# Retention followed by a gated unit: half of every second unit's convolution on VectorE, ScalarE and GpSimd, unit steps one pass later

## The chip, the cores and the metric

The kernel runs on one core of one Trainium2 chip. The metric is the device time of one execution in microseconds (us). The kernel before took 168.69 us as the median of three runs (168.61 to 168.87). Each profile shows one execution, and its durations belong to that execution alone.

## What is computed

The first part is retention (attention without a softmax, with a decay per head); the second a gated linear unit on its output, with a causal convolution of five taps as the gate:

```
scores = (q @ k.T) / sqrt(64)                 # 8 batches, 8 heads, 576 tokens, 64 per head
ret = scores * gamma[h] ** (i - j)            # for i >= j, else 0
x = (ret @ v), heads side by side             # 8 x 576 x 512
gate = sigmoid(sum over t of conv_w[t] * x shifted by 4 - t tokens)    # per channel
out = (gate * (x @ w_val)) @ w_out            # 8 x 576 x 512, float32
```

## The kernel before, in words

The tokens are cut into 36 chunks of 128: four full chunks for each batch, and, after every four batches, two chunks that hold the last 64 tokens of two batches each. Two successive chunks make a unit, so there are 18 units, numbered n; unit n has the chunks 2n and 2n+1. The decay is split into a factor per key token, put on V (`cast_v`, GpSimd, line 221), and a factor per query token, put on the result (`take_x`, VectorE, lines 331 and 337).

For a chunk the steps are these. `turn_k` (line 246) turns K on TensorE (line 241) into the PSUM bank `tps` and copies it to SBUF as `kt` (line 249). `scores` (line 280) multiplies K by Q into two banks; `masks` (line 289) evacuates each of the two with the causal mask. `carried` (lines 304, 310) adds what earlier chunks left in the state; `values` (line 321) adds masked scores times V; `take_x` stores the result as bf16 `xg`, with channels on the partitions, in four blocks of 128 channels. `update` (line 352) adds the chunk to the state and `take_state` (line 363, two ScalarE casts) copies the state to SBUF. The queries of a batch are loaded together, cast (`cast_q`, line 234), and turned by `turn_q` (lines 241 and 263) in four parts, one part a pass as a rule. In the main loop `turn_q` uses the same PSUM bank `tps` as `turn_k`; its pool has one buffer.

For a unit the steps are `conv` (line 385), `gate` (line 393), `value` (line 400, and the product with the gate on VectorE, line 403) and `project` (line 411, the copy on ScalarE, line 414, and the store, lines 417 and 420). `conv` runs five taps over four blocks as 64 x 64 diagonal matrices: 40 matmuls of 256 columns into two of the three PSUM banks of the pool `g`. `value` and `project` come in two halves, each with one bank of that pool.

The order is written out by hand, and every engine runs its instructions in that order. A prologue treats the chunks 0 to 3 and the units 0 and 1 with steps in single file and, where TensorE would idle, with matmuls on zeros (`keep_warm`, line 445). Then a loop over t = 4 to 37 (line 542) makes one pass a chunk: loads and casts ahead, `take_state(t)`, `scores(t+1)`, the first mask, `values(t)`, and then, in even passes, `take_x(t)`, the second mask, `conv(n)` and gates, `turn_k(t+2)`, two `value` halves with a `turn_q` between them; in odd passes `turn_k(t+2)` first, then `take_x(t)` and the second mask, then two `project` halves with a `turn_q` between them. Both end with `carried(t+1)` and `update(t+1)`. Unit n has its conv in pass 2n+2 and its projection in pass 2n+3. K is loaded by GpSimd's DMA queue four chunks ahead, V and Q by SyncE's (SP), which carries the stores too.

Of the kernel before, what the change touches and what calls it, by code (L numbers as in the profile page):

```python
# [13 lines left out]
F32 = mybir.dt.float32  # L14
BF16 = mybir.dt.bfloat16
# [6 lines left out]
def kernel(  # L22
# [48 lines left out]
    with tc.manual_schedule():  # L71
# [118 lines left out]
        mask_t = consts.tile([P, P], BF16, name="maskt")  # L190

        wvb = consts.tile([P, NP, NP, P], BF16, name="wvb")
        dg = consts.tile([P, NP, KC, 64], BF16, name="dg")
        cw = consts.tile([P, KC * NP], F32, name="cw")

# [23 lines left out]
        def cast_v(t, eng=nc.gpsimd):  # L219
            vb = bfp.tile([P, H, D], BF16, name="vb")  # L220
            eng.tensor_tensor(vb, loaded["v", *chunks[t]],  # L221
                                    gin[:, chunks[t][2], :].unsqueeze(2).to_broadcast([P, H, D]), op=ALU.mult)
            vbf[t] = vb
# [28 lines left out]
        def turn_q(job, copy=nc.scalar.copy, pool=None):  # L252
            ps = turned(qbf[job], pool)
            if job[0] == "own":
                qt = tp_sb.tile([P, NP, P], BF16, name="qt")
                qtd["own", job[1]] = qt
                dst = qt
            else:
                b, r = job[1:]
                if ("batch", b) not in qtd:  # L260
                    qtd["batch", b] = tp_sb.tile([P, NP, RQ, P], BF16, name="qtb", bufs=2)
                dst = qtd["batch", b][:, :, r, :]
            copy(dst, ps)  # L263
# [9 lines left out]
        def scores(t, spare=False):  # L273
            kt = ktd[t]
            s = [ps_g.tile([P, NP, P], F32, name="g") if spare else ps_s.tile([P, NP, P], F32, name=f"s{i}")
                 for i in range(2)]
            for pr in range(NP):
                for i in range(2):
                    r = slice(i * 64, i * 64 + 64)
                    nc.tensor.matmul(s[i][:, pr, :], lhsT=kt[r, pr, :], rhs=queries(t, r, pr),  # L280
                                     start=(pr == 0), stop=(pr == NP - 1), skip_group_check=True)
            sps[t] = s
# [84 lines left out]
        def xs(n, rows, blk, shift):  # L367
            kind, b, c = chunks[2 * n]
            x = xg[b // GB]
            if kind == "full":  # L370
                c0 = c * P + shift
                return x[rows, b % GB, blk, c0:c0 + 2 * P]
            c0 = NCH * P + shift
            return x[rows, :, blk, c0:c0 + TAIL]

        gps, gsb, zsb = {}, {}, {}

        def conv(n):
            g = [ps_g.tile([P, 2, 2 * P], F32, name="g") for _ in range(2)]
            lo, hi = slice(0, 64), slice(64, 128)  # L380
            for pr in range(2):
                a, b = 2 * pr, 2 * pr + 1
                for kk in range(KC):
                    for (rows, blk, cols, bank) in ((lo, a, lo, 0), (hi, b, lo, 1), (lo, b, hi, 0), (hi, a, hi, 1)):
                        nc.tensor.matmul(g[bank][cols, pr, :], lhsT=dg[rows, blk, kk, :], rhs=xs(n, rows, blk, kk),  # L385
                                         start=(pr == 0 and kk == 0), stop=(pr == 1 and kk == KC - 1),
                                         skip_group_check=True)
            gps[n] = g
            gsb[n] = []

        def gate(n, i):
            t = gp.tile([P, 2, 2 * P], F32, name=f"gate{i}")
            nc.scalar.activation(t, gps[n][i], AF.Sigmoid)  # L393
            gsb[n].append(t)

        def value(n, i):
            vps = ps_g.tile([P, 2, 2 * P], F32, name="g")
            for j in range(2):
                for o in range(NP):
                    nc.tensor.matmul(vps[:, j, :], lhsT=wvb[:, o, 2 * i + j, :], rhs=xs(n, slice(0, P), o, PAD),  # L400
                                     start=(j == 0 and o == 0), stop=(j == 1 and o == NP - 1), skip_group_check=True)
            z = gp.tile([P, 2, 2 * P], BF16, name=f"z{i}")
            nc.vector.tensor_tensor(z, gsb[n][i], vps, op=ALU.mult)  # L403
            zsb[n, i] = z

        def project(n, i):
            kind, b, c = chunks[2 * n]
            last = n == NT // 2 - 1
            o = ps_g.tile([P, DM], F32, name="g")
            for j in range(NP):  # L410
                nc.tensor.matmul(o, lhsT=zsb[n, j // 2][:, j % 2, i * P:(i + 1) * P], rhs=wob[:, j, :],  # L411
                                 start=(j == 0), stop=(j == NP - 1))
            ob = op_sb.tile([P, DM], F32, name="ob")
            nc.scalar.copy(ob, o)  # L414
            if kind == "full":
                c0 = (c + i) * P
                nc.sync.dma_start(out=out[b, c0:c0 + P, :], in_=ob)
            else:
                for j in range(2):
                    (nc.scalar if last and j else nc.sync).dma_start(out=out[b + 2 * i + j, NCH * P:S, :], in_=ob[j * TAIL:(j + 1) * TAIL])  # L420
# [40 lines left out]
        for (r, copy) in ((1, s_copy), (2, v_copy), (0, s_copy)):  # L461
            turn_q(("batch", 0, r), copy, ps_g)
        turn_q(("batch", 0, 3), v_copy)
        scores(0)
        masks(0, 0)
        masks(0, 1)
        turn_k(1, s_copy)
        cast_v(0)
        cast_v(1)
        load_keys(4)  # L470
        carried(0)
        update(0)
        take_state(0)
# [9 lines left out]
        prep_wv(s_copy, 0)  # L483
        prep_wv(g_copy, 1)
        cast_v(2)
        for t in sbl:
            nc.gpsimd.memset(t, 0.0)
        keep_warm(2, turn_bank=True)
        values(1)
        take_x(1)  # L490
# [7 lines left out]
        gate(0, 1)  # L498
        value(0, 0)
        cast_v(3)  # L500
        load_keys(5)
        load_wo()
        values(2)
        take_x(2)
        update(2)
# [9 lines left out]
        take_x(3)  # L515
        update(3)
        take_state(3)
        keep_warm(3, turn_bank=True)
        for (r, copy) in ((0, g_copy), (1, g_copy), (2, s_copy), (3, g_copy)):
            cast_q(("batch", 1, r), copy)  # L520
        cast_v(4)
        load_keys(6)
        conv(1)
        gate(1, 0)
        gate(1, 1)
        turn_k(4, s_copy)
        value(1, 0)
        turn_q(("batch", 1, 0), v_copy)
        turn_q(("batch", 1, 1), s_copy, ps_g)
        turn_q(("batch", 1, 2), v_copy)  # L530
        turn_q(("batch", 1, 3), s_copy, ps_g)
        carried(4)
# [1 line left out]
        scores(4)  # L534
        masks(4, 0)
        masks(4, 1)
        turn_k(5)
        value(1, 1)
        load_keys(7)
        cast_v(5)  # L540

        for t in range(4, NT + 2):
            n = t // 2 - 1
            unit = n < NT // 2
            odd = t % 2 == 1
            jobs = qjobs.get(t, [])
            for b in qload.get(t, []):
                load_queries(b)
            if ok(t + LA - 2):
                load(t + LA - 2)  # L550
            if ok(t + 4):
                load_keys(t + 4)
            if ok(t + 2):
                cast_v(t + 2)
            for job in qjobs.get(t + 1, []):
                cast_q(job)
            if ok(t):
                take_state(t)
            if ok(t + 1):
                scores(t + 1)  # L560
                masks(t + 1, 0)
            if ok(t):
                values(t)
                if not odd:
                    take_x(t)
            if ok(t + 1) and not odd:
                masks(t + 1, 1)
            if unit and not odd and n > 1:
                conv(n)
                gate(n, 0)  # L570
                gate(n, 1)
            if ok(t + 2) and t > 4:
                turn_k(t + 2)
            if ok(t) and odd:
                take_x(t)
            if ok(t + 1) and odd:
                masks(t + 1, 1)
            part = project if odd else value
            if unit and t > 4:
                part(n, 0)  # L580
            if t == 4:
                project(0, 0)
            if jobs:
                turn_q(jobs[0])
            if unit and t > 4:
                part(n, 1)
            if t == 4:
                turn_k(6)
                project(0, 1)
            for job in jobs[1:]:  # L590
                turn_q(job)
            if ok(t + 1):
                carried(t + 1)
                update(t + 1)
            if t == 5:
                nc.gpsimd.tensor_copy(mask_t, mask)
                nc.gpsimd.memset(mask_t[0:64, 64:128], 0.0)
# [1 line left out]
_INS = ['q', 'k', 'v', 'moe_w_val', 'moe_conv_w', 'moe_w_out']  # L599
_OUTS = [((8, 576, 512), 'float32')]  # L600
# [25 lines left out]
```

## Time and profile before

| | before |
|---|---|
| median of 3 runs | 168.69 us |
| the profiled execution | 168.61 us |
| its span, first to last instruction | 166.7 us |
| granted TensorE clock | 0.998 |
| data moved | 35.23 MB, mean 211 GB/s |
| K load, issue to landing | 4.1 / 7.0 / 10.8 us (least, median, most) |

The span begins with the first instruction and ends with the last; the 1.9 us that are left lie around it. Where engines are given as shares, TensorE's matmuls are PE and its weight loads PEld, VectorE is DVE, ScalarE ACT, GpSimd POOL. A line such as "L249 DVE COPY kt<-tps" names the line of the kernel, the engine, the operation, and the tile written and read. In a timeline the first number is the start and the second the duration in us; brackets at the end give the engine's idle time before the instruction and what ended it. In a chain a row has the start, the time in us, and the work.

### The profile page before, as it was taken

The page shows a single profiled execution, that of the slowest core. Times are in us where ns is not written, and L with a number is a line of the kernel's source. Part 1 is how long each engine was busy: PE and PEld are TensorE (multiplying, and loading weights), DVE is VectorE, ACT ScalarE, POOL GpSimd, SP SyncE. Part 2 cuts the span into 40 slices and gives each one's busy share as a digit, 9 for nine tenths or more (in the row PEclk, how much of TensorE's full clock was granted, in tenths as well). Part 3 has the DMA queues.
Part 4 walks back from the last instruction along what each step waited for, and adds up shares of the span by engine and source line. Part 5 has one row for each costly group of instructions (what it writes and reads, how often), then busy time and mean ns, then how long its engine had stood idle before and what let it go on. Part 6 is the DMA issues. An engine that isn't in the chain of part 4 may idle for free.

```text
span 166.7 us, 5543 instructions
## 1 busy us (share of the span) xinstructions
PE 153.5 (92%) x2297; PEld 110.2 (66%) x2297; DVE 114.2 (68%) x217; ACT 89.9 (54%) x183; POOL 99.4 (60%) x132
## 2 busy tenths in 40 slices
PE   6768878799999999999999999999999999999970
PEld 1344656556868777777868686868686877868630
DVE  6784673676677777768677777777777788686330
ACT  6934337446655557474546556565555563554430
POOL 7596999279699378675379286537977462000000
PEclk9999999999999999999999999999999999999999
DMA  5999999998999999999999999999999991303204
GB/s 112 301 264 253 294 213 288 226 162 238 275 263 287 247 236 214 174 258 267 267 163 246 268 274 188 216 285 289 233 259 187 212 236 42 130 0 130 97 33 126
DMA packets 93958, 35.23 MB, mean 211 GB/s; under 512 B 80090, under 2 KB 88814, under 8 KB 93934
## 3 DMA queue, kind: packets, MB, share of 16 engines
q1 hardware_dynamic: 57744, 29.63, 67.7%
q0 software_dynamic: 36000, 4.98, 44.0%
q8 instruction: 18, 0.29, 0.8%
q10 hardware_dynamic: 190, 0.27, 0.6%
q14 instruction: 6, 0.05, 0.1%
HBM read 30.42 MB, written 9.44 MB: 239 GB/s over the span
## 4 chain that ended last, share of the span: by engine, by line
PE 83%; ACT 4%; DVE 3%; POOL 3%; DMA 2%; issue 2%; ACTq 0%; DVEq 0%; POOLq 0%
PE g L400 18%; PE g L411 18%; PE g L385 13%; PE tps L241 10%; PE o L321 7%; PE s L280 7%; PE st L352 4%; PE o L304 3%; DMA fkc<-in_k_dram 2%; PE tps L445 1%; POOL dg L202 1%; ACT qtb L263 1%; DVE p L289 1%; DVE kt L249 1%; ACT ob L414 1%
## 5 line engine op out<-in xcount | busy, mean ns | idle before, releaser
L289 DVE TENSOR_TENSOR p<-s,maskq 128x512 bf16<-128x512 f32 x62 | 42.2, 685 | 17.6 <-PE s L280 17.5
L221 POOL TENSOR_TENSOR vb<-fvc,gin 128x512 bf16<-128x512 f32 x36 | 37.7, 1046 | 22.0 <-DMA fvc<-in_v_dram 9.0
L403 DVE TENSOR_TENSOR z<-gate,g 128x512 bf16<-128x512 f32 x36 | 24.7, 687 | 20.8 <-PE g L400 20.8
L400 PE MATMUL g<-xg,wvb 128*128 128x256 bf16 x288 | 36.9, 273 | 0.0
L411 PE MATMUL g<-wob,z 128*128 128x512 bf16 x144 | 36.5, 379 | 0.3 <-DVE z L403 0.3
L414 ACT COPY ob<-g 128x512 f32<-128x512 f32 x36 | 21.1, 585 | 28.3 <-PE g L411 28.0
L393 ACT ACTIVATE gate<-g 128x512 f32<-128x512 f32 x36 | 19.5, 594 | 19.1 <-PE g L385 19.1
L400 PEld LDWEIGHTS <-wvb 128*128 128x128 bf16 x288 | 26.6, 98 | 3.3 <-issue 0.6
L96 POOL DMA_DIRECT2D kb<-in_k_dram x30 | 28.4, 946 | 0.1
L234 POOL CAST qb<-fqb 128x512 bf16<-128x512 f32 x28 | 17.0, 620 | 13.1 <-DMA fqb<-in_q_dram 13.1
L385 PE MATMUL g<-xg,dg 64*64 64x256 bf16 x720 | 23.2, 271 | 0.0
L363 ACT CAST sbd<-st 64x256 bf16<-64x256 f32 x48 | 17.6, 366 | 8.8 <-PE st L352 8.3
L331 DVE TENSOR_TENSOR xg<-o,gout 128x512 bf16<-128x512 f32 x31 | 21.1, 681 | 1.3 <-PE o L321 1.3
L385 PEld LDWEIGHTS <-dg 64*64 64x64 bf16 x720 | 18.4, 106 | 2.3 <-issue 0.8
L411 PEld LDWEIGHTS <-z 128*128 128x128 bf16 x144 | 12.5, 98 | 10.4 <-DVE z L403 1.2
L263 ACT COPY qtb<-tps 128x512 bf16<-128x512 bf16 x24 | 14.1, 588 | 4.2 <-PE tps L241 4.2
L241 PE MATMUL tps<-ident,kb 128*128 128x128 bf16 x144 | 14.5, 224 | 0.8 <-DVE kb L216 0.8
L280 PE MATMUL s<-qtb,kt 64*128 64x128 bf16 x248 | 12.3, 219 | 2.5 <-DVE kt L249 1.1
L249 DVE COPY kt<-tps 128x512 bf16<-128x512 bf16 x33 | 14.0, 423 | 0.9 <-PE tps L241 0.7
L321 PE MATMUL o<-p,vb 128*64 128x128 bf16 x280 | 14.5, 225 | 0.0
L241 PEld LDWEIGHTS <-qb 128*128 128x128 bf16 x144 | 10.6, 98 | 5.4 <-issue 1.4
L352 PE MATMUL st<-vb,kb 128*128 128x128 bf16 x128 | 12.4, 219 | 0.7 <-POOL vb L221 0.7
(71 smaller groups left out, 142.0 us busy)
## 6 DMA issues: line engine op xcount, KB each, us to landing
fqb<-in_q_dram SPq DMA_DIRECT2D x8, 1024.0 KB, 9.3
fvc<-in_v_dram SPq DMA_DIRECT2D x32, 256.0 KB, 8.8
out_dram<-ob SPq DMA_DIRECT2D x32, 256.0 KB, 5.7
kb<-in_k_dram POOLq DMA_DIRECT2D x30, 128.0 KB, 7.5
wvf<-in_moe_w_val_dram SPq DMA_DIRECT2D x1, 1024.0 KB, 7.4
fqc<-in_q_dram SPq DMA_DIRECT2D x8, 128.0 KB, 5.2
fvc<-in_v_dram SPq DMA_DIRECT2D x8, 128.0 KB, 5.0
out_dram<-ob SPq DMA_DIRECT2D x6, 128.0 KB, 3.3
```

Source lines behind the costliest of these rows:

```text
L96: nc.gpsimd.dma_start(out=kb, in_=k[b, :, c * P:(c + 1) * P, :].rearrange("h p d -> p h d"))
L221: eng.tensor_tensor(vb, loaded["v", *chunks[t]], gin[:, chunks[t][2], :].unsqueeze(2).to_broadcast([P, H, D]), op=ALU.mult)
L241: nc.tensor.transpose(ps[:, pr, :], flat[:, pr * P:(pr + 1) * P], ident)
L280: nc.tensor.matmul(s[i][:, pr, :], lhsT=kt[r, pr, :], rhs=queries(t, r, pr), start=(pr == 0), stop=(pr == NP - 1), skip_group_check=True)
L289: nc.vector.tensor_tensor(p, sps[t][i], m.unsqueeze(1).to_broadcast([P, NP, P]), op=ALU.mult)
L321: nc.tensor.matmul(o[r, pr, :], lhsT=vb[:, 2 * pr + i, :], rhs=pt[t, i][:, pr, :], start=(fresh and pr == 0), stop=(pr == NP - 1), skip_gr ...
L331: nc.vector.tensor_tensor(by_token(x[:, bl, :, PAD + i0:PAD + i0 + P]), ops[t].rearrange("p o (r n) -> p o n r", r=RQ), by_token(gout[:, : ...
L385: nc.tensor.matmul(g[bank][cols, pr, :], lhsT=dg[rows, blk, kk, :], rhs=xs(n, rows, blk, kk), start=(pr == 0 and kk == 0), stop=(pr == 1 a ...
L400: nc.tensor.matmul(vps[:, j, :], lhsT=wvb[:, o, 2 * i + j, :], rhs=xs(n, slice(0, P), o, PAD), start=(j == 0 and o == 0), stop=(j == 1 and ...
L403: nc.vector.tensor_tensor(z, gsb[n][i], vps, op=ALU.mult)
L411: nc.tensor.matmul(o, lhsT=zsb[n, j // 2][:, j % 2, i * P:(i + 1) * P], rhs=wob[:, j, :], start=(j == 0), stop=(j == NP - 1))
L414: nc.scalar.copy(ob, o)
```

## The change

In the even units from 2 to 16, `conv` on TensorE does only the first pair of blocks (20 matmuls). Block 2 is computed by five VectorE instructions (`tap`), block 3 by five ScalarE activations with a scale per channel, of which four go to a tile `tap` (two buffers) and are added by GpSimd. Taps are spread over the passes 2n+1, 2n+2 and 2n+3; the last ones stand at the head of pass 2n+3. The gate of such a unit is made in four halves instead of two whole instructions, and its blocks 2 and 3 are in natural channel order, for which there are second copies of the weights (`wvn`, `won`). Every unit from 2 on has its conv and `value` one pass later (2n+3) and its `project` in 2n+4. `take_x` and the second mask stand directly behind `values` in every pass, and `turn_k` copies on ScalarE in the passes 2n+2 and 2n+3 of these units. In the prologue some steps trade places and engines.

```
+        wvn = consts.tile([P, NP, 2, P], BF16, name="wvn")
+        won = consts.tile([P, 2, DM], BF16, name="won")
...
+        aside = set(range(2, NT // 2, 2))
+        acc = {}
+
+        def tap(eng, n, i, kk):
+
+            if kk == 0:
+                acc[n, i] = gp.tile([P, 2 * P], F32, name=f"acc{i}")
+            x = xs(n, slice(0, P), 2 + i, kk)
+            a = acc[n, i]
...
+            w = cw[:, kk * NP + 2 + i:kk * NP + 3 + i]
+            if i == 1:
+
+                t = a
+                if kk:
+                    t = gp.tile([P, 2 * P], F32, name="tap")
...
+                nc.scalar.activation(t, x, AF.Identity, scale=w)
+                if kk:
+                    nc.gpsimd.tensor_tensor(a, a, t, op=ALU.add)
+            elif kk == 0:
+                eng.tensor_scalar(a, x, w, None, op0=ALU.mult)
+            else:
+                eng.scalar_tensor_tensor(a, in0=x, scalar=w, in1=a, op0=ALU.mult, op1=ALU.add)
 
         def conv(n):
...
-            for pr in range(2):
+            for pr in range(1 if n in aside else 2):
...
-            nc.scalar.activation(t, gps[n][i], AF.Sigmoid)
+            if n in aside:
+                nc.scalar.activation(t[:, 0, :], gps[n][i][:, 0, :], AF.Sigmoid)
+                nc.scalar.activation(t[:, 1, :], acc[n, i], AF.Sigmoid)
+            else:
+                nc.scalar.activation(t, gps[n][i], AF.Sigmoid)
...
         turn_q(("batch", 0, 3), v_copy)
+        cast_v(0, nc.vector)
         scores(0)
...
-        cast_v(0)
         cast_v(1)
-        load_keys(4)
+        for t in sbl:
+            nc.gpsimd.memset(t, 0.0)
...
         cast_v(2)
-        for t in sbl:
-            nc.gpsimd.memset(t, 0.0)
+        load_keys(4)
...
         cast_v(3)
+        load_wo()
         load_keys(5)
-        load_wo()
...
         take_state(3)
+        turn_k(4, s_copy)
         keep_warm(3, turn_bank=True)
-        for (r, copy) in ((0, g_copy), (1, g_copy), (2, s_copy), (3, g_copy)):
+        conv(1)
+        gate(1, 0)
+        gate(1, 1)
+        for (r, copy) in ((0, g_copy), (1, s_copy), (2, g_copy), (3, s_copy)):
             cast_q(("batch", 1, r), copy)
         cast_v(4)
         load_keys(6)
-        conv(1)
-        gate(1, 0)
-        gate(1, 1)
-        turn_k(4, s_copy)
         value(1, 0)
         turn_q(("batch", 1, 0), v_copy)
         turn_q(("batch", 1, 1), s_copy, ps_g)
+        value(1, 1)
...
         masks(4, 1)
+        project(0, 0)
         turn_k(5)
-        value(1, 1)
...
+            first = next((n for n in range(2, NT // 2) if t == min(2 * n + 3, NT)), None)
+            second = 0 if t == 4 else 1 if t == 5 else next((n for n in range(2, NT // 2) if t == min(2 * n + 4, NT + 1)), None)
+            on_act = any(t in (2 * n + 2, 2 * n + 3) for n in aside)
...
+            for n in aside:
+                if t == 2 * n + 3:
+                    tap(None, n, 1, 4)
+                    tap(nc.vector, n, 0, 3)
+                    tap(nc.vector, n, 0, 4)
...
             if ok(t):
                 values(t)
-                if not odd:
-                    take_x(t)
-            if ok(t + 1) and not odd:
+                take_x(t)
+            if ok(t + 1):
                 masks(t + 1, 1)
-            if unit and not odd and n > 1:
-                conv(n)
-                gate(n, 0)
-                gate(n, 1)
+            if first is not None and t < NT:
+                conv(first)
+                gate(first, 0)
+                gate(first, 1)
             if ok(t + 2) and t > 4:
-                turn_k(t + 2)
-            if ok(t) and odd:
-                take_x(t)
-            if ok(t + 1) and odd:
-                masks(t + 1, 1)
-            part = project if odd else value
-            if unit and t > 4:
+                turn_k(t + 2, s_copy if on_act else v_copy)
+            for n in aside:
+                if t == 2 * n + 1:
+                    tap(None, n, 1, 0)
+                    tap(None, n, 1, 1)
+                    tap(nc.vector, n, 0, 0)
+                if t == 2 * n + 2:
+                    tap(None, n, 1, 2)
+                    tap(None, n, 1, 3)
+                    tap(nc.vector, n, 0, 1)
+                    tap(nc.vector, n, 0, 2)
+            part, n = (value, first) if first is not None and t < NT else (project, second)
+            if n is not None and t != 4:
                 part(n, 0)
             if t == 4:
-                project(0, 0)
+                project(0, 1)
             if jobs:
                 turn_q(jobs[0])
...
+            if t == NT:
+                conv(first)
+                for i in range(2):
+                    gate(first, i)
+                for i in range(2):
+                    value(first, i)
+            if t == 4:
+                nc.gpsimd.dma_start(out=won, in_=moe_w_out[2 * P:4 * P, :].rearrange("(i p) n -> p i n", p=P))
             if t == 5:
                 nc.gpsimd.tensor_copy(mask_t, mask)
                 nc.gpsimd.memset(mask_t[0:64, 64:128], 0.0)
+                for i in range(2):
+                    nc.gpsimd.tensor_copy(wvn[:, :, i, :], wvf[:, :, (2 + i) * P:(3 + i) * P])
```

## The prediction

> **What bounds the kernel now.** I read four views: the shares by engine with the 40 slices, the busy times in stretches, the chain that ended last, and the timeline of a pair of passes of the main loop.
>
> ```profile
> PE 153.5 (92%) x2297; PEld 110.2 (66%) x2297; DVE 114.2 (68%) x217; ACT 89.9 (54%) x183; POOL 99.4 (60%) x132
> PE   6768878799999999999999999999999999999970
> DVE  6784673676677777768677777777777788686330
> ACT  6934337446655557474546556565555563554430
> ```
>
> TensorE (PE) is full from the ninth slice to the end; VectorE (DVE) and ScalarE (ACT) stay near seven and five tenths. In the stretches PE is busy 16.00 of 16.00 us everywhere from 64 to 144 us, and idle for only 2.0 us between 28 and 48 us. The chain, cut to one pair of passes, says what PE does in that time:
>
> ```profile
> 143.17 1.22 PE g L385 x40
> 144.38 0.33 PE tps L241 x4
> 144.72 0.87 PE g L400 x8
> 145.59 0.22 PE tps L241 x4
> 145.81 0.87 PE g L400 x8
> 146.69 0.22 PE o L304 x4
> 146.91 0.22 PE st L352 x4
> 147.13 0.33 PE s L280 x8
> 147.46 0.34 PE o L321 x8
> 147.81 0.33 PE tps L241 x4
> 148.13 0.86 PE g L411 x4
> 149.00 0.22 PE tps L241 x4
> 149.22 0.86 PE g L411 x4
> ```
>
> It is PE piece after piece: the even pass takes 4.6 us with the convolution (1.22 us) and two value products, the odd one 3.2 to 3.4 us with two projections. PE is the bound, so conv time taken from it is worth its full length as long as nothing makes PE wait. What could is seen in the timeline of one odd pass, which starts at 76.67:
>
> ```profile
> 77.15 0.69 DVE L289 TENSOR_TENSOR p<-s,maskt 128x512 bf16<-128x512 f32 x1
> 77.34 0.40 PE L241 MATMUL tps<-ident,kb 128*128 128x128 bf16 x4
> 77.77 0.42 DVE L249 COPY kt<-tps 128x512 bf16<-128x512 bf16 x1
> 78.11 0.68 DVE L331 TENSOR_TENSOR xg<-o,gout 128x512 bf16<-128x512 f32 x1
> 78.44 0.39 PE L241 MATMUL tps<-ident,qb 128*128 128x128 bf16 x4
> 78.64 0.58 ACT L414 COPY ob<-g 128x512 f32<-128x512 f32 x1 [1.07 <-PE g L411]
> 78.71 0.68 DVE L289 TENSOR_TENSOR p<-s,maskt 128x512 bf16<-128x512 f32 x1
> 79.12 0.59 ACT L263 COPY qt<-tps 128x512 bf16<-128x512 bf16 x1
> ```
>
> The K chunk and the Q job are turned through one PSUM bank, tps (a pool of one buffer). The Q transposes (1.77 us after the pass began) can't start before kt has been copied out of it (1.52 us after): a margin of 0.25 us. That such a wait stops PE, the prologue shows:
>
> ```profile
> 27.84 0.59 ACT L249 COPY kt<-tps 128x512 bf16<-128x512 bf16 x1
> 28.48 0.38 PE L241 MATMUL tps<-ident,qb 128*128 128x128 bf16 x4 [0.46 <-ACT kt L249]
> ```
>
> [...]
>
> **The change, part by part.** All sums are made against the profiled execution: 168.61 us, with a span of 166.7; the median of the runs is 168.69.
>
> *Conv.* Eight of 18 units run 20 instead of 40 conv matmuls: 8 x 1.22/2 = -4.9 us on PE.
>
> *Added work.* [...] DVE and GpSimd have room. The copy of kt moves from DVE to ACT in two passes of every four.
>
> Call the passes of the loop A (t=2n+1, n even: full conv of unit n-1, first taps), B (2n+2: project n-1), C (2n+3: half conv of n), D (2n+4: project n).
>
> *D: the order on DVE.* take_x and the second mask now stand ahead of kt in every pass; in passes with projections (the odd ones of before) kt stood ahead of them. DVE starts these 0.60 to 0.62 us apart: p at 0.48 after the pass begins, x 1.10, second p 1.70, kt 2.30 to 2.72, bank free 2.76. PE is at the Q transposes at 1.77, so it waits 0.99 us. In A the full conv (1.22 us) covers this; in B kt is on ACT and ready at 1.69. D with a Q job occurs at t=8, 12, 16, 20, 24, 28, 32: 7 x 0.99 = +6.9. Bounds 0.8 to 1.05 each.
>
> *C: the queue on ACT.* In B, ACT runs kt from 1.10, then two taps, and the two projection copies with the Q copy between them (3 x 0.48): 1.10+0.49+0.80+1.45 = 3.84, 0.45 into C (B lasts 3.4). In C come a tap (0.40), the state casts (0.74), four gate halves (1.20), and only then kt: it starts at 2.79 and ends at 3.38, bank free 3.42. PE is ready at 3.00 (75.03-72.03) less 0.61 of conv, 2.39. Wait: 1.03. If taps queue at 0.28 it is 0.65; without overlap on ACT 1.5. C with a Q job: t=11, 15, 19, 23, 27, so 5 x 1.03; and t=7, where ACT has no projection copies behind it but the second add may wait for a Q load, 0.9 (0.7 to 1.1). Sum +6.1. At t=31 and 35 there is no Q job and no wait. Queued behind ACT's taps are the state casts, the gates and the copies; behind GpSimd's adds, its K loads and casts of V and Q. K loads land in a median of 7.0 us (at most 10.8) and have some 9 to 11 us, so I put these at nothing; GpSimd's wvn casts (2 x 0.6) likewise.
>
> *Start and passes 4 to 6.* cast_v(0) on DVE ends at about 11.4 instead of 12.08, and the chain up to the fourth state gains 0.5 us. Then turn_k(4) stands ahead of keep_warm, which uses the same bank, so conv(1) waits for kt(4) behind the state cast on ACT: about 26.5 instead of 25.53. K chunk 4 is now issued at 17.5 instead of 13.08 and is due at 24.4, with a 7.0 us landing just in time (late by 0 to 0.8). ACT's two Q casts come behind the gates; scores(4) at 31.7 instead of 30.66, with value(1,1) done. project(0,0) fills the hole of 1.7 us behind scores(4). Pass 5 has D's order (+1.0) and ACT taps ahead of its copies; pass 6, with no unit in it, is a chain of three turns through the bank with their ACT copies and two taps, 4.0 us long against 1.9 of PE work. Pass 7 begins at about 45.3 instead of 44.95 although the 2.96 us of unit 2 (1.22+1.74) aren't in front of it any more: 0.4+2.96 = +3.4. Bounds +1.5 to +4.5: each turn and landing may be off by half a microsecond. The won load (512 KB) is taken at nothing; 2 us at 239 GB/s if the K loads behind it are late, which is within these.
>
> *End.* Project(16) follows value(16) at once and waits for z (0.70 plus 0.08) behind two of its own matmuls (0.43): +0.3 (0 to 0.6). SP's outputs move with their passes; their loads are issued six passes ahead, taken at nothing.
>
> Sum: -4.9 + 6.9 + 6.1 + 3.4 + 0.3 = +11.8, so 168.6 + 11.8 = 180.4 us.
>
> **The rivals.** *PE stays the bound (not slower).* If kt is out of the bank before 1.77 us in D and 2.39 in C, and in passes 5 and 6 too, only the conv saving counts: -4.9, +0.3 at the end, +0.6 at the start: 164.6. It decides at exactly the 0.25 us margin seen above; against it speaks that DVE would have to finish three 0.69 us operations and a copy in 1.3 us. *Only DVE's order binds.* ACT's halves overlap better and C's waits stay near 0.3: 168.6-4.9+6.9+1.8+3.0+0.3 = 175.7, down to 172.5 if the start also goes well. *GpSimd couples loads to PE.* There are two tap buffers, so ACT's later taps wait for GpSimd's adds, which stand behind casts waiting for Q loads (13.1 us in 5 waits, up to 3.7). Where the first cast of a batch falls into a B pass (t=6, 10), or K comes late, that adds 2.5 us each time: about +6, 186. That the change doesn't do what it says isn't open: its PE stream has 160 conv matmuls fewer.
>
> **How the numbers follow.** Likeliest 0.74: 180.4, own range 174.7 (all low bounds: -4.9+5.6+3.9+1.5+0) to 184.8 (all high: -4.9+7.35+8.6+4.5+0.6). Only DVE's order: 0.11. GpSimd: 0.06. PE the bound: 0.09, of which 0.02 lands within 0.2%, about what a measurement of this kernel can tell from no change. So faster 0.07, same 0.02, slower 0.91. The range 172.5 to 185.5 takes in the first two cases and leaves out about 0.15 with the others.
>
> **What would show it.** Right: the list of waits has the Q transposes on PE waiting for DVE's kt about seven times and for ACT's kt about six times, by about 1 us each; PE is idle near a tenth of the time in the main loop; conv groups of 20 take 0.61; in D the DVE order p, x, p, kt. Wrong: kt's copies end before PE has done the first projection or value product, PE stays at 16.00 of 16.00, or the longest new waits are for DMA on GpSimd.

## The result and the profile after

The changed kernel takes 199.65 us (median of 4 runs, 199.14 to 200.08), the kernel before 168.78 in the same comparison: a ratio of 1.1825, 95% interval 1.1792 to 1.1859. The forecast was 180.4, with a range up to 185.5. The direction was right; the loss is 30.9 us instead of 11.8. The profiled execution took 199.69 us, its span is 198.0. Some executions of a kernel run over 1.5% longer, in a slower state, and are left out of every time and ratio here.

The page of the changed kernel: busy time by engine, then two rows of the slices.

```profile
PE 159.8 (81%) x2137; PEld 110.5 (56%) x2137; DVE 139.6 (71%) x244; ACT 114.7 (58%) x254; POOL 123.3 (62%) x165
...
PE   5868857877889879978992999298965999699990
...
PEclk9999999997899999999999699969996799999999
```

PE is no longer full. Two slices show a busy share of two tenths, others of five or six, and the clock that PE is granted drops to six or seven tenths in the same places or just behind. PE has 160 matmuls fewer and yet is busy for 6 us more (153.5 before): it works slower for part of the time. The list of waits (total, times, longest) names what stops it:

```profile
PE tps L244 <- ACT kt L252: 15.5, 7, 3.9
...
ACT gate L424 <- DVE acc L405: 10.9, 7, 3.0
...
PE tps L244 <- DVE kt L252: 5.6, 6, 1.4
```

The first and the last line are the two waits of the forecast, seven and six times. But the one for ACT's kt comes to 15.5 us instead of about 6, and the line between them was in no step of mine: ACT's gates wait up to 3.0 us for VectorE's accumulator. The groups (busy us, mean ns) say why:

```profile
L401 POOL TENSOR_TENSOR acc<-acc,tap 128x256 f32<-128x256 f32 x32 | 24.6, 768 | 46.8 <-ACT tap L399 45.9
...
L405 DVE SCALAR_TENSOR_TENSOR acc<-xg,cw,acc 128x256 f32<-128x256 bf16 x32 | 32.2, 1005 | 0.9
```

I had put a tap on VectorE at 0.42 us, an estimate of mine. It takes 1.005 us on average; single ones lie between 0.479 and 2.791. The timeline around a C pass, which starts at 101.21, shows one of the long ones (some of the VectorE, ACT and GpSimd lines, and the PE line that waits):

```profile
100.14 6.03 DVE L405 SCALAR_TENSOR_TENSOR acc<-xg,cw,acc 128x256 f32<-128x256 bf16 x4
...
103.01 0.94 POOL L96 DMA_DIRECT2D kb<-in_k_dram  x1
...
103.97 1.06 POOL L224 TENSOR_TENSOR vb<-fvc,gin 128x512 bf16<-128x512 f32 x1
104.96 0.61 POOL L237 CAST qb<-fqb 128x512 bf16<-128x512 f32 x1
...
106.09 0.68 DVE L292 TENSOR_TENSOR p<-s,maskq 128x512 bf16<-128x512 f32 x1
106.20 0.42 ACT L424 ACTIVATE gate<-acc 128x256 f32<-128x256 f32 x1 [2.98 <-DVE acc L405]
...
107.10 0.57 ACT L252 COPY kt<-tps 128x512 bf16<-128x512 bf16 x1
...
107.72 0.38 PE L244 MATMUL tps<-ident,qb 128*128 128x128 bf16 x4 [3.88 <-ACT kt L252]
```

Four taps take 6.03 us. The last of them starts at 103.38 (the chain shows it with 2.80 us) and ends at 106.17, 0.60 us after GpSimd's cast. Behind it on VectorE stand p, x and the second p; behind it through the gate on ACT stands kt, and behind kt PE, idle for 3.88 us. Such a pause costs twice. After the same pause in the C pass near 150 us the matmuls are slow (usual here are 0.38 us for the transposes and 0.60 for a group of four value matmuls):

```profile
150.56 0.58 PE L244 MATMUL tps<-ident,qb 128*128 128x128 bf16 x4 [3.86 <-ACT kt L252]
150.94 1.06 PE L434 MATMUL g<-xg,wvb 128*128 128x256 bf16 x4
```

The granted clock is at half from 108.60 to 112.01, from 129.08 to 132.49 and from 149.56 to 156.39 us, in or just behind the three long pauses. Each row here is a stretch of time with its length, the busy us and (x) the instructions of PE, PEld, DVE, ACT and POOL, then the granted clock, the DMA share and GB/s:

```profile
105.19:108.60 3.41, 0.88 (x10) 0.80 (x10) 3.37 (x5) 1.93 (x5) 3.39 (x5) 1.00 1.50 152
108.60:112.01 3.41, 3.41 (x34) 2.43 (x32) 2.05 (x4) 0.86 (x3) 1.98 (x3) 0.50 0.72 46
```

PE was busy for 0.88 of the 3.41 us ahead of the slow stretch; the last 2.53 us of the pause lie in them. Between 43.75 and 47.16 us PE was busy for 1.57 of 3.41 us, with several waits below 1 us, and 3.41 us at half clock followed. Single waits of 1.2 us (passes 11 and 15; around the first PE was busy for 2.20 of 3.41 us, from 67.64 to 71.05) left no such mark: the clock stays at 1.00. In the run below with kt ahead and the taps in, three pauses of 2.4 us occur, and after two of them the clock is halved for 3.41 us.

The clue was in the trace of the kernel before. There, two identical operations with two SBUF inputs that prepare the diagonals on VectorE (dg, 320 elements) took 491 and 1017 ns, beside two of the same form on GpSimd (here the durations are least, median and most, in ns):

```profile
L202 DVE TENSOR_TENSOR dg<-cw,id x2: 491/754/1017, 6.5 to 6.9; 128x320 bf16<-128x320 f32 x2
L202 POOL TENSOR_TENSOR dg<-cw,id x2: 966/996/1026, 6.6 to 7.6; 128x320 bf16<-128x320 f32 x2
```

VectorE's first one started 0.05 us ahead of GpSimd's first, its second while that ran. I had given the taps one price instead of asking what else they could wait for.

### The profile page after: what moved, and what is told of

Same layout as the page of the kernel before. It is cut to its first block, busy times and chain, and to the rows that moved or that the text cites. A ratio compares the mean times of both kernels' runs of the same rounds, so it can differ in the third digit from the quotient of the medians.

```text
span 198.0 us, 5308 instructions
## 1 busy us (share of the span) xinstructions
PE 159.8 (81%) x2137; PEld 110.5 (56%) x2137; DVE 139.6 (71%) x244; ACT 114.7 (58%) x254; POOL 123.3 (62%) x165
## 4 chain that ended last, share of the span: by engine, by line
DVE 36%; PE 28%; ACT 14%; DMA 8%; issue 4%; SPq 4%; POOL 3%; ACTq 0%; DVEq 0%; POOLq 0%
DVE acc L405 15%; DVE p L292 9%; PE g L434 6%; PE g L414 6%; PE g L446 5%; DVE z L437 5%; DMA kb<-in_k_dram 4%; DVE xg L334 4%; DMA fvc<-in_v_dram 4%; ACT gate L426 4%; PE tps L244 3%; SPq L78 3%; PE s L283 3%; ACT gate L424 2%; ACT kt L252 2%
## 5 line engine op out<-in xcount | busy, mean ns | idle before, releaser
L401 POOL TENSOR_TENSOR acc<-acc,tap 128x256 f32<-128x256 f32 x32 | 24.6, 768 | 46.8 <-ACT tap L399 45.9
L446 PE MATMUL g<-wob,z 128*128 128x512 bf16 x112 | 33.1, 386 | 0.7 <-DVE z L437 0.7
L405 DVE SCALAR_TENSOR_TENSOR acc<-xg,cw,acc 128x256 f32<-128x256 bf16 x32 | 32.2, 1005 | 0.9
L434 PE MATMUL g<-xg,wvb 128*128 128x256 bf16 x224 | 31.3, 280 | 0.0
L244 PE MATMUL tps<-ident,qb 128*128 128x128 bf16 x124 | 12.1, 221 | 22.1 <-ACT kt L252 15.5
L244 PEld LDWEIGHTS <-qb 128*128 128x128 bf16 x144 | 10.9, 100 | 29.5 <-issue 25.8
L434 PEld LDWEIGHTS <-wvb 128*128 128x128 bf16 x224 | 20.9, 100 | 3.1 <-issue 0.8
L414 PE MATMUL g<-xg,dg 64*64 64x256 bf16 x560 | 19.4, 277 | 0.0
L426 ACT ACTIVATE gate<-g 128x512 f32<-128x512 f32 x20 | 10.9, 595 | 13.2 <-PE g L414 13.2
L237 POOL CAST qb<-fqb 128x512 bf16<-128x512 f32 x27 | 16.6, 621 | 2.3 <-DMA fqb<-in_q_dram 2.3
L266 ACT COPY qtb<-tps 128x512 bf16<-128x512 bf16 x24 | 14.1, 586 | 5.6 <-PE tps L244 5.6
L399 ACT ACTIVATE tap<-xg,cw 128x256 f32<-128x256 bf16 x32 | 15.6, 510 | 2.4 <-POOL acc L401 2.4
L414 PEld LDWEIGHTS <-dg 64*64 64x64 bf16 x560 | 14.3, 107 | 2.5 <-issue 1.0
```

Source lines behind the costliest of these rows:

```text
L244: nc.tensor.transpose(ps[:, pr, :], flat[:, pr * P:(pr + 1) * P], ident)
L401: nc.gpsimd.tensor_tensor(a, a, t, op=ALU.add)
L405: eng.scalar_tensor_tensor(a, in0=x, scalar=w, in1=a, op0=ALU.mult, op1=ALU.add)
L434: nc.tensor.matmul(vps[:, j, :], lhsT=w, rhs=xs(n, slice(0, P), o, PAD), start=(j == 0 and o == 0), stop=(j == 1 and o == NP - 1), skip_gr ...
```

## The experiments

Theory, formed from this trace: a VectorE operation with two SBUF inputs and a GpSimd operation that reads SBUF exclude one another. The expectations call it the port theory, and what the two would share a port or an interface; the runs show which operations are held and for how long, not by what. Rivals: the taps only stand in the wrong place of VectorE's queue; or kt does (queues, not a lock). Times below are medians in us, with the ratio to the kernel before, measured on the same chip, in brackets.

**Leave out one side each.** First the VectorE taps after the first (their sum is then incomplete), then the GpSimd adds instead (likewise):

```
-            else:
-                eng.scalar_tensor_tensor(a, in0=x, ...)
```


> Leaves out four of the five VectorE taps of block 2 (the first, a product without a sum, stays), so that the output of these units lacks them; all else as in the changed kernel. Port theory (VectorE's scalar_tensor_tensor waits for GpSimd's reads, which makes half a gate late, then kt on ScalarE, then the Q transposes, and TensorE's clock falls after the long idle): the time falls to 178 to 181 us, what the prediction's sum had with a tap of 0.42 us; the Q transposes wait about 1 us each for kt on ScalarE instead of 2.2, the granted clock is above 0.99. Queue theory (order on VectorE and ScalarE alone, the length of the taps is hidden): 195 us or more.


```
-                if kk:
-                    nc.gpsimd.tensor_tensor(a, a, t, op=ALU.add)
```


> Leaves out GpSimd's adds of block 3 (ScalarE's taps stay, their sum isn't made). Port theory: GpSimd reads for 24.6 us less, but its casts of V and Q stay; scalar_tensor_tensor falls from a mean of 1005 ns to about 700, the time to 185 to 193 us. If only the adds block VectorE: mean near 480 and 181 us or less. Queue theory: the mean stays, 196 us or more.

Measured: 184.06 (1.0894) and 184.04 (1.0866). Without the taps 15.6 us go, somewhat less than I had put on the theory; a start that is slower than forecast (below) would account for that. PE's waits for the bank are then 13.0 us, what the forecast had for its C and D steps together, 6.1 + 6.9:

```profile
PE tps L244 <- ACT kt L252: 6.5, 7, 2.2
PE tps L244 <- DVE kt L252: 6.5, 8, 0.9
```

Without the adds the taps are all there, and take 591 ns on average instead of 1005; I had expected about 700 ns, and 185 to 193 us. So most of what holds the taps comes with GpSimd's adds. Not all of it is direct: the taps of 2.79 us, which end behind an issue, a product and a cast, occur once instead of three times. Leaving the adds out shifts GpSimd's other work too.

**Queues alone.** The changed order with nothing taken aside (full convolutions, kt on the engines of the change), and the change with kt copied ahead of x, the second mask and the gates:

```
-        aside = set(range(2, NT // 2, 2))
+        aside = set()
```


> No unit is set aside: no taps, adds, half gates or second weights in use, full conv on TensorE; the later unit steps, take_x and the second mask ahead of kt, kt on ScalarE in two passes of four, and the prologue stay as in the changed kernel. From the prediction's terms: D 6.9, C 0.6 in six passes (kt behind whole gates: 3.62 against 3.00), start 2.6, end 0.3: 180 to 184 us, though TensorE has 4.9 us more to do than in the changed kernel. If the unit steps one pass later cost much by themselves: above 188. If the order costs nothing: below 172.


```
+            if no_conv and ok(t + 2) and t > 4:
+                turn_k(t + 2, s_copy if on_act else v_copy)
             if ok(t):
                 take_x(t)
...
                 conv(first)
+                if ok(t + 2) and t > 4:
+                    turn_k(t + 2, s_copy if on_act else v_copy)
                 gate(first, 0)
...
-            if ok(t + 2) and t > 4:
-                turn_k(t + 2, s_copy if on_act else v_copy)
```


> The changed kernel with kt copied out of the bank first: ahead of take_x and the second mask where a pass has no conv, ahead of the gates on ScalarE where it has one. Queue theory: both bank waits go, 168 to 174 us. Port theory: the waits of D go (about 6 us), but in C VectorE is still stuck in scalar_tensor_tensor, so that the masks and the gate products come late and TensorE waits for them in the next pass: 185 to 193 us.

Measured: 184.59 (1.0922, from two runs only) and 186.52 (1.1024). The first is at the upper end of what I expected and hardly above it; the later steps and the new prologue cost more than the +3.7 that I had for them (below). The second brings 13 us of 31. PE then doesn't wait for kt any more but for x (7.4 us in 3 waits, behind the taps), and the taps still take 1013 ns. The rival that kt's place is all falls.

**The cost by itself.** To the kernel before nine stretches were appended. In each, VectorE runs six taps, and GpSimd a list of operations, both started together. This and the second run of its kind are single executions, and what is compared are stretches of one trace.

> The kernel before, with nine short stretches appended, in each of which VectorE runs six operations of the form of the taps (128x256 bf16 times a column plus an accumulator) while GpSimd runs a list of operations, both started together. Theory (two SBUF inputs share an interface with GpSimd's reads): alone 0.48 us each; beside GpSimd adds, casts and the V products the VectorE ones are held to the end of a GpSimd operation, so single ones of 0.8 to 2.5 us; beside memsets 0.48; with the accumulator in PSUM or with the one-input product 0.35 to 0.5, undisturbed. Open within the theory: beside GpSimd's DMA issues. [...] Rival (the operation is slow by itself when its accumulator was just written): 0.8 and more with GpSimd idle too.

The timeline of five of them (alone; four adds; three V products; three DMA issues; four adds, with the accumulator in PSUM):

```profile
165.91 3.09 DVE L642 SCALAR_TENSOR_TENSOR bacc<-xg,cw,bacc 128x256 f32<-128x256 bf16 x6
...
169.83 4.46 DVE L642 SCALAR_TENSOR_TENSOR bacc<-xg,cw,bacc 128x256 f32<-128x256 bf16 x6
170.00 3.49 POOL L629 TENSOR_TENSOR bsum<-bsum,btap 128x256 f32<-128x256 f32 x4
...
184.06 3.40 POOL L635 TENSOR_TENSOR bdst<-bsrc,gin 128x512 bf16<-128x512 f32 x3
184.07 5.24 DVE L642 SCALAR_TENSOR_TENSOR bacc<-xg,cw,bacc 128x256 f32<-128x256 bf16 x6
...
190.14 3.09 DVE L642 SCALAR_TENSOR_TENSOR bacc<-xg,cw,bacc 128x256 f32<-128x256 bf16 x6
190.19 2.71 POOL L637 DMA_DIRECT2D bk<-in_k_dram  x3
...
193.37 3.12 DVE L642 SCALAR_TENSOR_TENSOR g<-xg,cw,g 128x256 f32<-128x256 bf16 x6
193.38 3.12 POOL L629 TENSOR_TENSOR bsum<-bsum,btap 128x256 f32<-128x256 f32 x4
```

Alone a tap takes 0.48 us. Beside adds four of the six take 0.83, and beside three V products three take 1.15 to 1.31: in these stretches the two engines take turns, one operation each, and a held tap ends some 0.28 us after the operation that holds it. Beside casts the six take 4.20 us. Beside memsets, which only write, they take 3.09, as alone. With the accumulator in PSUM nothing is held (six in 3.12 us). So the operation isn't slow by itself. I was wrong on the one-input product: it too is held, 0.69 to 0.77 us instead of 0.35. Why, no run shows.

DMA issues alone hold nothing (six taps in 3.09 us beside three issues). What then made a tap of 2.79 us that starts during one? A list of add, issue, V product, cast, issue had given a single tap of 1.92 us, so the issue was tried with different followers:

> The kernel before with six more stretches appended: six VectorE operations of the form of the taps beside (1) a DMA issue and a memset on GpSimd, (2) an issue and a V product, (3) issue, V product, cast into another tile, issue, (4) V product, cast, V product into three tiles, (5) the same three into one tile, (6) list 3 with the accumulator in PSUM. Theory: an issue alone holds nothing, but operations queued behind one another without a dependency keep the interface, so in (1) all 0.48; in (2) one of about 1.5 to 1.9; in (3) one of 2.3 to 2.8, as in the changed kernel; in (4) one of about 2.5 to 3; in (5) they alternate, three of 0.8 to 1.3; in (6) all 0.49. Rival (the hold ends with each GpSimd operation, and the 2.79 us had another cause): in (3) and (4) none over 1.4.

The stretch with an issue and a V product:

```profile
170.68 4.72 DVE L634 SCALAR_TENSOR_TENSOR bacc<-xg,cw,bacc 128x256 f32<-128x256 bf16 x6
...
171.07 0.88 POOL L632 DMA_DIRECT2D bk<-in_k_dram  x1 [0.30 <-issue]
171.96 1.05 POOL L630 TENSOR_TENSOR bd<-bsrc,gin 128x512 bf16<-128x512 f32 x1
```

The tap that starts at 171.20 takes 2.11 us: it is held from the issue to the end of the product behind it. With a memset behind the issue all six take 0.48. So it looks as if the reading operation behind an issue holds the taps from soon after the issue begins, here within 0.13 us. The run without the adds shows a limit of this: a tap that began 0.36 us into an issue with a product behind it took 0.48 us, and there the product's last wait ended only 0.16 us after the tap had begun. My idea that operations without a dependency hold the taps for the whole queue was wrong: a cast behind the product let a tap in between (2.18 and 0.71 us), and so did three independent operations in a row (1.37, 0.71, 1.15). In the changed kernel the tap also waited for the cast, and ended 0.60 us after it, not 0.28; and the first taps of five passes (1.30 to 1.40 us) waited for a cast and for the add behind it. Why these taps weren't let in between isn't settled.

**All the work, without the hold.** The accumulator of the taps in the unused half of the bank tps, in the order of the change and with kt ahead:

```
-                acc[n, i] = gp.tile([P, 2 * P], F32, name=f"acc{i}")
+                acc[n, i] = gp.tile([P, 2 * P], F32, name=f"acc{i}") if i else tb[:, 2 * P:4 * P]
```


> The changed kernel with all of its work and order; only the accumulator of the VectorE taps lies in the unused half of the bank in which K and Q are turned, so that those operations have one SBUF input. Theory (the taps are held by GpSimd's reads over the shared interface): each tap 0.49 us, none over 0.6, and the time falls to that of the run without them, 184 us (183 to 186). Rival (what costs is that VectorE has the taps to do, or that they stand ahead of p and x): the taps still take 0.5 us x 32 = 16 us of VectorE, and the time stays at 190 or more. Should the matmuls into the other half of the bank wait for the taps, PE shows waits for acc, and the run tells nothing.

> As the run before it in this call, and kt copied ahead of x, the second mask and the gates: the change with both of its faults mended and all of its work done. Theory: the two costs add (15.6 and about 11 us), so 173 to 175, what the run without the taps gave, still slower than before by the start and the end. Rival (they are one queue: with the taps in place something else is late): 177 to 184.

Measured: 197.20 (1.1644) and 187.24 (1.1027), both far from what the theory had. The proviso came true in both: transposes and taps, which now lie in one tile, are ordered against each other, and PE waits 9.9 us for taps. The totals say nothing. The group of the taps does say something: with all the work done, and GpSimd's adds beside them, no tap is over 0.49 us, and the C passes t=23 and 27 fall from 9.36 and 9.55 us to 4.90.

By group (busy us, mean ns):

```profile
L407 DVE SCALAR_TENSOR_TENSOR tps<-xg,cw,tps 128x256 f32<-128x256 bf16 x32 | 15.6, 487 | 9.0 <-ACT qtb L268 7.2 <-ACT qt L268 1.2
```

To keep VectorE as long in the same places without the hold, each tap after the first was then replaced by an operation with one SBUF input (a sum of neighbours; the tap is left out), in the order of the change and with kt ahead:

```
-                eng.scalar_tensor_tensor(a, in0=x, scalar=w, in1=a, ...)
+                eng.tensor_reduce(a[:, 0:P], x.rearrange("p (n r) -> p n r", r=2), ...)
```


> The changed kernel, in which each VectorE tap after the first is replaced by an operation with one SBUF input on the same 128x256 elements (a sum over pairs of neighbours, so the tap itself is left out), in the same place and written to the same accumulator. Theory (GpSimd's reads hold operations with two SBUF inputs): these take about 0.42 to 0.48 us each, none is held, and the time is that of the run without the taps plus little, 184 to 187 us, with PE's bank waits at about 13 us. Rival (any 0.5 us operation in these places delays p, x and kt that much): 191 or more.

> The run before it in this call with kt ahead of x, the second mask and the gates as well. If the two costs add and nothing else binds: 173 to 176, as without the taps (173.6). Rival (with taps in VectorE's queue the move of kt brings less): 178 or more.

Measured: 183.81 (1.0829, 1.0756 to 1.0903) and 172.88 (1.0186, 1.0098 to 1.0274). In the first one, by group, and PE's waits for the bank:

```profile
L401 POOL TENSOR_TENSOR acc<-acc,tap 128x256 f32<-128x256 f32 x32 | 23.2, 727 | 32.3 <-ACT tap L399 31.5
L408 DVE TENSOR_REDUCE acc<-xg 128x128 f32<-128x256 bf16 x28 | 11.7, 417 | 0.7
...
PE tps L244 <- DVE kt L252: 6.5, 8, 0.9
PE tps L244 <- ACT kt L252: 5.3, 7, 0.9
```

GpSimd's adds are all done (23.2 us, against 24.6 in the change), and 0.417 us on VectorE in the place of each tap costs nothing that can be measured: the time is that of the run with the taps left out. This settles the main question. It isn't that VectorE has more to do, nor where the taps stand, but that they are held. With kt ahead too, the time is that of the next run, which leaves the taps out. So the two costs are both there, and about add: the hold is worth 16.8 us in the order of the change and 14.1 with kt ahead, a difference that these intervals can't tell from none.

**Start, later steps, and the conv saving.** Four runs: kt ahead and no VectorE taps; this with K chunk 4 loaded and turned at about its old place; the kernel before with half of the convolution in the even units (the second pair of blocks is left out); and the changed order with kt ahead and nothing aside.

> Leaves out the VectorE taps after the first and copies kt ahead of x, the second mask and the gates. If the waits for the bank (13.0 us without the taps) are simply the price of kt's place in the queues, they go and nothing comes in their place: 184.1 - 13.0 = 171 us (170 to 173). Rival (PE waits for the next thing in those queues, the gates or x, as with the taps in, where the same move brought only 13 us of 31): 175 to 181.


```
         cast_v(1)
+        load_keys(4)
...
         cast_v(2)
-        load_keys(4)
...
-        turn_k(4, s_copy)
         keep_warm(3, turn_bank=True)
         conv(1)
+        turn_k(4, s_copy)
```


> As the run before it in this call, and with K chunk 4 loaded at its old place ahead of the state memsets, and turned behind conv(1). If the prologue loses its time to this chunk's late load and its turn (1.36 + 0.67 us of PE's waiting in the changed kernel), 2.0 to 2.7 us less than that run; if to the Q casts and copies behind the gates, 0 to 0.7 less.


```
-            for pr in range(2):
+            for pr in range(1 if n in halved else 2):
```


> The kernel before with its own order, and only PE's part of the change: in the eight even units the convolution of the second pair of blocks is left out and nobody does it (both gate halves are taken from the first pair, by four ACT operations). If PE is the bound there and the conv is worth its length, 168.7 - 8 x 0.61 = 163.8 us (163.3 to 164.6). Rival (other engines are close behind and hide a part): 165.5 to 168.

> The changed order and prologue with nothing taken aside (full convolutions, no taps), and kt copied ahead: what the later unit steps and the new prologue cost by themselves. If the conv saving is worth its length in the mended kernel, 173.6 + 3 to 4.9 = 176.6 to 178.5. Rival (after the late start the loads of V set the pace of passes 7 to 10 anyway, and the saving is hidden there): 174 to 176.

Measured: 173.50 (1.0199), 173.93 (1.0251), 166.49 (0.9808, 0.9748 to 0.9868) and 176.12 (1.0381, 1.0302 to 1.0461). The halved convolution gains 1.9%, about 3.2 us, not 4.9. In its trace the halved passes take 4.34 us instead of 4.64, so 0.30 of 0.61 comes through. I put that down to the Q transposes, which in that order then wait for kt: the margin of 0.25 us. The test copied kt ahead in these passes:

```
+                if ahead and ok(t + 2):
+                    turn_k(t + 2)
                 if not odd:
                     take_x(t)
...
-            if ok(t + 2) and t > 4:
+            if ok(t + 2) and t > 4 and not ahead:
                 turn_k(t + 2)
```


> The kernel before with halved convolutions in the even units (the other half is left out, as in the earlier run of this kind), and in these passes kt copied ahead of x and the second mask. If the earlier run kept only half of the saving because the Q transposes waited 0.3 us for kt, these passes go from 4.34 to 4.03 us where loads are in time, and the time from 166.5 to 164 to 165. Rival (the loads of V set the pace, so what is gained is waited for later): 166 to 167.

Measured: 166.76 (0.9811). The passes become 4.20 to 4.22 us between 73 and 123 us, not the 4.03 that I had for them, and the time stays, as the rival had it. Its reason isn't shown. Pass 10 waits 0.85 us for a K load and takes 5.12 us instead of 4.64, so in the early passes the loads are just in time (K's, not V's); but the run without the move has a like wait, 0.88 us in pass 9. The span of the profiled execution is 0.6 us shorter (164.8 against 165.4), its time is not, and why that is stays open. Early K4 gained 0.66 us at scores(4) and lost it at the next late K load, where PE waits 2.2 us instead of 1.4, so the total is the same within the intervals.

## Why the prediction was wrong, point by point

The ladder of runs puts a size on each term (differences of ratios times 168.7 us; the intervals of single ratios are some 0.7 to 0.9% wide to each side, so each term is good to about 2 us, the sum of the terms to less):

```
term                               forecast  measured  from
start and end (order, prologue)      +3.7      +6.4    order only, kt ahead: 1.0381
conv and the other added work        -4.9      -3.3    one-input taps, kt ahead: 1.0186
kt's place in the queues (C, D)     +13.0     +10.9    one-input taps, order of the change: 1.0829
VectorE taps held by GpSimd           0       +16.8    the change: 1.1825
sum                                 +11.8     +30.8
```

The length of single passes in the middle of the loop (from one group of score matmuls to the next) shows the same:

```
pass        forecast  changed  one-input taps  and kt ahead
C, t=23       5.06      9.36        5.02           4.12
D, t=24       4.4       4.54        4.33           3.40
A, t=25       4.6       4.42        4.42           4.42
B, t=26       3.4       3.40        3.40           3.40
```

- *Wrong: "DVE and GpSimd have room."* This is the step that failed. The 0.42 us that I had for a tap on VectorE was an estimate that no run shows. I priced the tap like p (0.69 us for 512 elements), which reads PSUM and one SBUF tensor; but a tap reads two SBUF tensors, beside a GpSimd that is busy 60% of the time. The taps measured 1.005 us, 0.48 of it their own length (alone, in the appended stretches). I gave the unknown operation one price and no upper end, so the range couldn't take in the loss.
- *Where the 16.8 us are.* Of 16.6 us between the two spans (198.0 and 181.4), the three C passes t=19, 23 and 27 have 12.6: 8.79, 9.36 and 9.55 us against 5.06, 5.02 and 5.02. About 9 of that are PE's longer pauses (3.9 instead of 0.8 us); the rest is a remainder, and I put it down to the slower clock behind them. In t=11 and 15 the last tap had started before the issue, and the pass was only 0.56 us longer.
- *Right: the waits for the bank.* Six to eight waits on either engine, 13.0 us without the taps and 11.8 with the one-input operation; with kt ahead they go, at a gain of 10.9 us. C and D had the lengths that the sums gave.
- *Right: ACT.* The sum for C takes queued taps at 0.40 us each and four gate halves at 1.20; these were estimates of mine, and no trace of the kernel before shows them. In the changed kernel queued taps start 0.40 to 0.42 us apart, and in pass 7 kt starts 1.15 us after the first gate half (50.19 and 51.34). By themselves taps take 0.510 us, gate halves 0.375 and 0.412. GpSimd's adds, which I had put at 0.55, an estimate too, take 0.73 undisturbed; only ACT's taps waited for that, and twice. Once it was 1.95 us, in pass 7, where the add stood behind a Q load; that is the coupling of the third rival, and it stayed a single case. The other time it was 0.41 us, near 166 us, behind an add that a VectorE tap had lengthened.
- *Too small: the start.* K chunk 4, issued at 17.86, is turned only at 26.36, after PE idled 1.36 us for it; I had a landing of 7.0 us, and it took 8.5. Its turn and copy hold the warm-up matmuls for 0.67 more. Pass 7 begins at 47.12 instead of 45.3. That is 1.8 of the 2.7 us that this term is above its forecast. And the start differs between executions. In the runs without the adds and with the order only (kt ahead or not), these waits are followed by 3.41 us at half clock from about 28 us on, and pass 7 begins at 47.65 to 48.43; with kt ahead and one-input operations there is no such stretch, and it begins at 46.40. So the terms for the start and for the conv, which are told apart by two such runs, are the least sure.
- *Too large: the conv saving.* As PE time it was right (halved passes have 0.61 us less to do), but 3.3 us came through. Waits at kt and for K loads in the early passes are seen in the traces; that they took the third that is missing isn't shown.
- *The rivals.* "PE stays the bound" needed kt early: with kt ahead and no hold the change still is 1.9% slower. None of the three had a blocked engine in it.

No run that does all of the work beat the kernel before, and the ladder says why: with both faults gone the later steps and the prologue cost about twice what the convolution saves (+6.4 against -3.3 us).

## What to carry to other kernels

Before work is moved to VectorE, count the SBUF inputs of each operation and look at what GpSimd reads at that time. In these runs operations with one of two inputs in PSUM were not held (0.49 us), nor was a sum with a single input (0.417), while a product with a single input was. Operations with two inputs in SBUF took up to six times their own length beside a busy GpSimd (2.79 us against 0.48). Two equal operations of very different length in the trace of before (491 and 1017 ns) are worth an explanation before anything is priced. And follow what stands behind a lengthened operation to PE: a pause of nearly 4 us was paid again in clock each time (half clock for 3.41, 3.41 and 6.83 us), one of 2.4 us in two of three cases.

## What the runs showed of the hardware that was not expected

- A DMA issue on GpSimd alone doesn't hold VectorE (six taps in 3.09 us beside three issues), nor with a memset behind it; with a V product behind it a tap that starts in the issue is held through both, 2.11 us.
- A product of one SBUF input (256 elements, bf16 to fp32) takes 0.69 to 0.77 us beside GpSimd adds instead of 0.35; a sum over pairs, of the same input, stayed at 0.417 in the kernel.
- GpSimd pays as well: beside taps its casts took 0.68 to 0.82 us instead of 0.61, its adds 0.78 to 0.90 instead of 0.72.
- The granted clock was halved for 3.41 us after a stretch of the same length in which PE had been busy for 1.57 us (in the change, to 47.16 us). After one with 2.20 us busy (to 71.05) it stayed at 1.00.
